# Casting q and k from a packed order: contiguous reads and strided writes in place of strided reads and contiguous writes

## The chip, the cores and the metric

The kernel runs on one core of a Trainium2 chip. Its time is the device time of one execution in microseconds (us). A core has TensorE (PE; its weight loads are listed apart as PEld), VectorE (DVE), ScalarE (ACT), GpSimd (POOL) and SyncE (SP). Each takes its instructions from a queue of its own in order, and they wait for one another with semaphores. SP issues most of the DMAs, GpSimd those of the FFN's weights, and ScalarE a few at the start.

## The reference

Two stages, for 4 batches, 8 heads, 768 tokens and a head dimension of 64.

First an attention that picks chunks. Keys are cut into 24 chunks of 32; for each chunk the minimum and the maximum of every key component are taken. A query's upper bound for a chunk is `sum(max(q*kmin, q*kmax))` over the 64 components. Chunks that lie behind the query's own are barred, the best 6 of the others are kept, and softmax attention runs over the kept chunks with a causal mask.

```
ub = sum(maximum(q * k_min, q * k_max), axis=-1)   # then the causal bar
sel = the 6 chunks with the highest ub
attn = softmax(where(sel & causal, q @ k.T / 8, -1e9))
x = (attn @ v) as 3072 tokens x 512
out = (silu(xn @ w_gate) * (xn @ w_val)) @ w_out,   xn = x / rms(x) * rms_g
```

Then a gated FFN with RMS norm: 3072 tokens, 512 wide, 1536 inside. The output is 3072 x 512 in float32.

## The kernel before

The work is cut into 12 blocks, each of one batch and 256 tokens (`ORDER`); the first four blocks are token block 0 of batches 0 to 3, where only 8 chunks exist. A block has two groups `g` of four heads. Blocks are counted from 0 here.

**Order of the work.** Every step (a few instructions on one engine) is registered with `plan.op` or `flex` (where more than one engine could do it), with estimated costs and a due time from the list `DUE`. `Plan.run` simulates engines and DMA rings with these estimates and writes out one order for each engine before the kernel is built. The order in which steps are issued thus follows from the estimates, not from what happens on the chip. The planner also writes filler matmuls (`keep_busy`, L1245) into PE's queue where it expects a gap in the first 60 us.

**The packed order.** For the blocks in `PACKED` (0, 1, 2) q and k are loaded so that one partition row `r` (of 32) holds 8 neighbouring tokens `j`: token = 8 r + j. VectorE's transpose of 32x32 squares (`turn`, L794) then leaves `kT` and `qT` as `[128, 2, 256]` float32 with the 256 columns in the order (j, r): a packed order. For the other blocks token = 32 j + r, so the same transpose leaves the columns in natural order.

From `kT` and `qT`, for each group:

- `half` (L801 on ScalarE, L802 on GpSimd) casts to bf16 into `kb` and `qb`, in natural token order. These feed the score matmuls `S` (L922). In packed blocks it reads `order(...)`, that is r outside and j inside, so that neighbouring reads are 32 float32 elements apart, and writes one after the other.
- `ext` (L809, VectorE) takes the minimum and the maximum of each chunk into `kx`; `dk` (L815) subtracts; `bd` (L834) places the results in `BO`, the weights of the upper bound.
- `relu` (L888, GpSimd or VectorE) writes max(q, 0) of the last 64 tokens over the first part of `qraw`, in packed blocks in natural order, reading with the same stride.
- `upper_first` (L698, PE) multiplies `qT` and that relu with `BO` for the blocks of token block 0. Its moving operand is read in the order (r, j): from `qT` with a rearranged pattern, from the relu as it lies.

What follows: `ubn`, `top`, `mk`, `mt` and `swap` on VectorE (some of `swap` on ScalarE, L759) pick chunks and build the mask; score matmuls and mask matmuls (L922, L933), exponentials (L972, ScalarE), the causal triangle (L942, GpSimd), values (L998, PE), division (L1013, L1017, VectorE) into `xnat`; then the norm: squares (L1034, ScalarE), the root (L1040, L1042, GpSimd), scaling `xs` (L1068 ScalarE, L1066 VectorE), transposes on PE (L1078) and `xsT` (L1087 ScalarE, L1091 VectorE). The FFN takes `xsT` as its moving operand (L1122), then tanh (L1129), products (L1133, L1141, L1144) and the projection (L1169). The FFN of block i is issued beside the attention of later blocks.

Buffers: `kT` and `qT` have 2, `qraw` 3, `qb` 5, `kb` 17; PSUM has four `F` banks and two `S` pairs. The weights come in nine loads of 512 KB from GpSimd's queue, the first of them behind the `dk` of block 0, with L942 between them.

Of the kernel before, what the change touches and what calls it, by code (L numbers as in the profile page):

```python
# [11 lines left out]
ACT = mybir.ActivationFunctionType  # L12
# [395 lines left out]
def kernel(  # L408
# [41 lines left out]
    def at(key):  # L450
        return store[plan.pool_of[key]][plan.slot[key]]
# [46 lines left out]
    VE, SE, GE, TE, SY = nc.vector, nc.scalar, nc.gpsimd, nc.tensor, nc.sync  # L498
# [13 lines left out]
    PACKED = {0, 1, 2}  # L512
# [27 lines left out]
    def flex(name, alts, pri, **kw):  # L540
        e = next(iter(alts))
        o = plan.op(name, e, *alts[e], pri, **kw)
        o.alts = alts
        return o
# [102 lines left out]
    def pick(i, gs):  # L647
        b, m = ORDER[i]
        w = 64 if m == 0 else BLK
# [10 lines left out]
        def own_(key):  # L660
            return [key + (g,) for g in gs]
# [4 lines left out]
        def bank():  # L666
            return [at(x)[:, 0:n * 32 * nj].rearrange("p (g n) -> p g n", g=n) for x in ub]
# [16 lines left out]
        def upper_first():  # L684
            for k_, g in enumerate(gs):
                qT, qr, bo = sides[i, g][0:3]
                x = at(qT)[:, g]
                if i in PACKED:
                    x = x.rearrange("p h (j r) -> p h r j", r=32)[:, :, 32 - w // 8:].rearrange(
                        "p h (c r) j -> p h c r j", c=2)  # L690
                else:
                    x = x[:, :, BLK - w:].rearrange("p h (c r j) -> p h c r j", c=2, j=8)
                qs = [x, qr().rearrange("p h (c r j) -> p h c r j", c=2, j=8)]
                d = at(bo)
                for t in range(4):
                    for hp in range(2):
                        for c in range(2):
                            TE.matmul(bank()[hp][64 * c:64 * (c + 1), k_].rearrange("p (r j) -> p r j", j=8),  # L698
                                      d[64 * hp:64 * (hp + 1), t, :],
                                      qs[t // 2][64 * hp:64 * (hp + 1), t % 2, c],  # L700
                                      start=(t == 0), stop=(t == 3),
                                      skip_group_check=True)

        reads = []
        for g in gs:
            qx, qr, bd, qR, qraw, crossed = sides[i, g]
            reads += [bd, qx, qR, qraw] + crossed
            if m:
                reads += [bd + (x,) for x in range(m + 1)] + [qx + (g,)]
        o = plan.op(f"upper{tag}", "PE", (0.52 if m else 0.49) * n, (0.52 if m else 0.49) * n + 0.165,  # L710
                    upper if m else upper_first, base + 3, reads=reads, writes=ub, takes=[(x, "F") for x in ub])
        o.mode = "sq"

        def rows(key):
            return at(key)[:, g0:g1].rearrange("p g h j c -> p (g h) j c")

        def flat(key):
            return at(key)[:, g0:g1].rearrange("p g h j c -> p g h (j c)")[:, :, :, 0:32 * nj]

        turned = ((0.37 if m else 0.17), (0.65 if m else 0.25))[n - 1]  # L720
# [14 lines left out]
        def top():  # L735
# [10 lines left out]
            out=rows(mk)[:, :, 0:nj], in0=rows(ubn)[:, :, 0:nj],  # L746
# [3 lines left out]
            out=flat(mtd), in_=flat(mk)), base + 3, reads=[mk] + own_(mk), writes=own_(mtd),  # L750
# [17 lines left out]
    def job(i, g):  # L768
        b, m = ORDER[i]
        J = (b, m, g)  # L770
        w = 64 if m == 0 else BLK
# [6 lines left out]
        def turned(nm):  # L778
            return at(kT) if nm == "k" else at(qT)[:, g]

        packed = i in PACKED

        def order(x):

            return x.rearrange("p h (j r) -> p h r j", r=32) if packed else x

        def natural(x):
            return x.rearrange("p h (r j) -> p h r j", r=32) if packed else x
        bd = ("BD", b)

        def turn(nm):
# [6 lines left out]

        def half(nm):
            T, hb = kT if nm == "k" else qT, (nm + "b", *J)  # L800
            act = lambda: SE.activation(out=natural(at(hb)), in_=order(turned(nm)), func=ACT.Copy)  # L801
            pool = lambda: GE.tensor_copy(natural(at(hb)), order(turned(nm)))  # L802
            flex(f"half {nm}{J}", {"ACT": (0.54, 0.63, act), "POOL": (0.57, 0.61, pool)},
                 base + 2 - first, reads=[T, T + (g,)], writes=[hb], takes=[(hb, nm + "b")])

        turn("k")
        half("k")
        for n, op in enumerate((ALU.min, ALU.max)):
            plan.op(f"ext{n}{J}", "DVE", 0.585, 0.67, lambda n=n, op=op: VE.tensor_reduce(  # L809
                out=at(kx)[:, g, n], in_=at(kT).rearrange("p h (j c x) -> p h c j x", j=8, x=4)  # L810
# [21 lines left out]
        for n in range(0 if m else 2):  # L832
            def put(eng, n=n):
# [8 lines left out]
                 writes=[bo + (n,)], takes=[] if n else [(bo, "BO")])  # L842
        turn("q")
        half("q")
        qR, qx = ("qR", *J), ("QX", b, m)

# [6 lines left out]
        if m:  # L853
# [6 lines left out]
            if i in BYRING:  # L860
                crossed = [qx + (n, "x") for n in range(4)]
                for n, (lo, hi, p_, t) in enumerate(CROSS if g == NG - 1 else ()):
                    o = plan.op(f"qm{n}({b}, {m})", "SP", 0.57, 0.57,
                                lambda lo=lo, hi=hi, p_=p_, t=t: SY.dma_start(
                                    out=at(qx)[hi:hi + 32, :, p_, BLK - w:], in_=at(qT)[lo:lo + 32, :, t, BLK - w:]),
                                base - 20, reads=[qT, qx] + [x + (y,) for x in (qT, qx) for y in range(NG)],
                                writes=[qx + (n, "x")])
# [9 lines left out]
        def qr():  # L877
            return at(qraw)[:, g].rearrange("p j h d -> p (j h d)")[:, 0:2 * w].rearrange(
                "p (h s) -> p h s", h=2)

        def relu(eng):
            def go():
                o, x = qr(), at(qx if m else qT)[:, g]
                if packed:
                    o, x = o.rearrange("p h (r j) -> p h r j", j=8), order(x)[:, :, 32 - w // 8:]
                else:
                    x = x[:, :, BLK - w:]
                eng.tensor_scalar(out=o, in0=x, scalar1=HUGE, scalar2=0.0, op0=ALU.min, op1=ALU.max)  # L888
            return go
# [21 lines left out]
        def unit(kg, sc, tiles, masked):  # L911

            kbt, qbt = at(("kb", b, kg, g)), at(qb)
            s = [at(x) for x in sc]
            for e, q0, q1, c0 in tiles:
                ks = slice(P * e, P * (e + 1))
                jq = max(j0, q0 // 64)
                mask = masked and jq < q1 // 64
                for t in range(2):
                    for a in range(4):  # L920
                        r = slice(32 * a, 32 * (a + 1))
                        TE.matmul(s[a // 2][:, a % 2, c0:c0 + q1 - q0],  # L922
                                  kbt[r, t, ks], qbt[r, t, q0:q1],
                                  start=(t == 0), stop=(t == 1 and not mask), skip_group_check=True)
                for d in range(2) if mask else ():
                    for a in range(4):
                        r = slice(32 * a, 32 * (a + 1))
                        hp = a // 2
                        c = hp if d == 0 else 1 - hp
                        o = s[hp][:, a % 2, c0:c0 + q1 - q0].rearrange(  # L930
                            "p (j c r) -> p j c r", c=2, r=CH)[:, jq - q0 // 64:, c, :]
                        mv = (at(mtd)[r, g, hp] if d == 0 else at(mto)[r, g])[:, jq - j0:nj, :]
                        TE.matmul(o, chunkrow[r, BLK * kg + P * e:BLK * kg + P * (e + 1)], mv,  # L933
                                  start=False, stop=(d == 1), skip_group_check=True)
# [11 lines left out]
        for kg in [m] + list(range(m)):  # L946
# [11 lines left out]
            for part, tiles, c0, c1, pe, occ, lat in parts:  # L958
# [4 lines left out]
                o = plan.op(f"scores{J}{kg}{part}", "PE", pe, pe + 0.2,  # L963
                            lambda kg=kg, sc=sc, tiles=tiles, masked=masked: unit(
                                kg, sc, tiles, masked), pri,
                            reads=[("kb", *jk), qb] + ([mtd, mto, mtd + (g,), mto + (g,), "chunkrow"] if masked else []),
                            writes=sc, takes=[(x, "S") for x in sc])
                o.mode = "row"
                for hp in range(2):
# [3 lines left out]
                                out=at(pt)[:, hs, c0:c1], in_=at(x)[:, :, c0:c1], func=ACT.Exp,  # L973
# [13 lines left out]
        for s in range(2):  # L987
# [3 lines left out]
            def values(s=s, av=av, nkb=nkb):  # L991
                o = at(av)[:, 0:4 * (D + 1)].rearrange("p (a d) -> p a d", a=4)
                for kb_ in range(nkb):
# [3 lines left out]
                    for a in range(4):  # L997
# [7 lines left out]
            o = plan.op(f"values{J}{s}", "PE", 0.129 * nkb, 0.129 * nkb + 0.16, values, pri,  # L1005
                        reads=have + [("VX", b, x, g) for x in range(m + 1)],
                        writes=[av], takes=[(av, "F")])
            o.mode = "full"

            def view(av=av):  # L1010
# [7 lines left out]
                        out=at(xn)[:, g * 256:(g + 1) * 256].rearrange("p (a d) -> p a d", a=4),  # L1018
# [260 lines left out]
```

## Time and profile before

| | us |
|---|---|
| runs | 299.69, 300.06, 302.14; median 300.06 |
| profiled execution: span from first to last instruction | 297.4 |
| the same with what lies around the span | not recorded for that execution; the runs' median lies 2.7 above its span |
| PE busy / ScalarE busy / GpSimd busy | 282.5 / 216.7 / 155.6 |
| twelve packed casts: ten on ScalarE, two on GpSimd | 1.06 to 1.15 each |
| six packed relus on GpSimd | 0.40 each |

How rows are read. A group of instructions has the source line, the engine, the operation, output<-input with shapes, and the count; then busy time and the mean of one in ns; then the idle time of the engine ahead of these instructions and what ended it. Rows of the timeline begin with the start and the duration in us; neighbouring instructions of the same kind are merged. The chain of waits begins at the last instruction and is followed back to what released each step. Rows on waiting say who waited for whom, and for how long in total, how often, and at most.

### The profile page before, as it was taken

The numbers are of one execution on the slowest core, as the hardware profiler recorded it, in microseconds if no ns is written. First come the engines' busy times: TensorE is split into PE (matmuls) and PEld (weight loads), VectorE is DVE, ScalarE is ACT, GpSimd is POOL, SyncE is SP. The second block draws the span as 40 slices with busy tenths as digits, with TensorE's granted clock in tenths as the row PEclk, the third lists the DMA queues.
The fourth block names the chain that finished last, engine by engine and source line by source line (L and its number), as shares of the span: only waits on it lengthen the run. The fifth ranks groups of instructions, "written<-read, shape, count | busy, mean of one in ns | idle before, by whom it ended". The sixth has DMA issues, their size and how long they took to land.

```text
span 297.4 us, 11418 instructions
## 1 busy us (share of the span) xinstructions
PE 282.5 (95%) x4672; PEld 213.4 (72%) x4672; DVE 217.1 (73%) x623; ACT 216.7 (73%) x372; POOL 155.6 (52%) x266
## 2 busy tenths in 40 slices
PE   7879999999999996999999999899999999999994
PEld 7548777657858854878767787488688778678763
DVE  6987774977998998888999999679356454456430
ACT  4897877688979876987985797677587668565331
POOL 4885858755976864475583276538044114214120
PEclk9999999999999999999999999999999999999998
DMA  7999998755676656654768576511014021011011
GB/s 188 208 204 206 255 197 163 159 130 134 141 194 154 144 136 103 149 100 110 205 135 162 108 193 150 133 40 39 0 57 55 1 82 30 2 73 35 2 71 71
DMA packets 86388, 35.08 MB, mean 118 GB/s; under 512 B 74816, under 2 KB 81728, under 8 KB 86336
## 3 DMA queue, kind: packets, MB, share of 16 engines
q1 hardware_dynamic: 80736, 29.12, 42.6%
q0 software_dynamic: 4752, 4.72, 9.4%
q8 instruction: 36, 0.59, 0.8%
q10 hardware_dynamic: 848, 0.53, 0.7%
q14 instruction: 16, 0.13, 0.2%
HBM read 28.58 MB, written 6.29 MB: 117 GB/s over the span
## 4 chain that ended last, share of the span: by engine, by line
PE 76%; DMA 9%; DVE 4%; ACT 4%; SPq 3%; POOL 1%; issue 1%; DVEq 0%; POOLq 0%; ACTq 0%
PE F L1122 39%; PE F L1169 18%; PE S L922 6%; PE F L998 6%; PE F L680 3%; SPq L528 3%; PE S L933 2%; DMA xsT<-xs 2%; DMA qraw<-in_q_dram 2%; DMA vraw<-in_v_dram 2%; DMA kraw<-in_k_dram 2%; DVE kx L809 1%; POOL hh L1144 1%; DVE m L739 1%; ACT th L1129 1%
## 5 line engine op out<-in xcount | busy, mean ns | idle before, releaser
L972 ACT ACTIVATE pt<-S 128x1024 bf16<-128x1024 f32 (+3 forms) x104 | 85.6, 857 | 19.7 <-PE S L933 18.2
L1144 POOL TENSOR_TENSOR hh<-tg,vs 128x512 bf16<-128x512 bf16 x48 | 55.7, 1164 | 42.6 <-ACT vs L1141 22.9
L1133 DVE SCALAR_TENSOR_TENSOR tg<-th,F 128x512 bf16<-128x512 bf16 x72 | 48.4, 680 | 39.3 <-ACT th L1129 33.7
L1122 PE MATMUL F<-xsT,wg 128*128 128x256 bf16 (+1 forms) x608 | 72.6, 267 | 3.7 <-DVE xnat L1017 1.7
L1122 PE MATMUL F<-xsT,wv 128*128 128x256 bf16 (+1 forms) x608 | 72.4, 267 | 0.6 <-DMA xsT<-xs 0.3
L1169 PE MATMUL F<-wo,hh 128*128 128x512 bf16 (+1 forms) x300 | 68.5, 371 | 1.8 <-POOL hh L1144 0.6
L1122 PEld LDWEIGHTS <-wg 128*128 128x128 bf16 x608 | 55.6, 98 | 13.5 <-issue 2.7
L1122 PEld LDWEIGHTS <-wv 128*128 128x128 bf16 x608 | 55.2, 98 | 9.7 <-DMA vraw<-in_v_dram 0.8
L1129 ACT ACTIVATE th<-F 128x512 bf16<-128x512 f32 x72 | 42.5, 598 | 19.7 <-PE F L1122 17.4
L942 POOL TENSOR_SCALAR_AFFINE_SELECT pt<-pt 128x512 bf16<-128x512 bf16 x48 | 32.2, 674 | 32.3 <-ACT pt L972 31.7
L1169 PEld LDWEIGHTS <-hh 128*128 128x128 bf16 x300 | 27.7, 98 | 28.4 <-issue 1.8
L1141 ACT ACTIVATE vs<-F 128x512 bf16<-128x512 f32 x48 | 28.7, 598 | 13.2 <-PE F L1122 10.1
L922 PE MATMUL S<-qb,kb 32*128 32x256 bf16 (+1 forms) x800 | 32.8, 253 | 2.3 <-ACT qb L801 2.0
L809 DVE TENSOR_REDUCE kx<-kT 128x16 f32<-128x512 f32 x48 | 30.4, 664 | 0.0
L998 PEld LDWEIGHTS <-pt 128*128 128x128 bf16 x672 | 24.8, 98 | 3.1 <-issue 0.3
L998 PE MATMUL F<-VX,pt 128*128 128x65 bf16 x672 | 26.6, 194 | 0.2 <-ACT vs L1141 0.2
L922 PEld LDWEIGHTS <-kb 32*128 32x128 bf16 x800 | 13.9, 92 | 15.0 <-issue 14.4
L933 PE MATMUL S<-mtd,chunkrow 32*128 32x128 bf16 (+2 forms) x384 | 20.5, 203 | 0.2 <-issue 0.2
L933 PE MATMUL S<-mto,chunkrow 32*128 32x128 bf16 (+2 forms) x384 | 19.9, 203 | 0.0
L1017 DVE TENSOR_TENSOR xnat<-F,rden 128x256 bf16<-128x256 f32 x48 | 19.2, 415 | 0.7
L933 PEld LDWEIGHTS <-chunkrow 32*128 32x128 bf16 x768 | 18.5, 93 | 1.2 <-issue 0.4
L1034 ACT ACTIVATE junk<-xnat 128x512 bf16<-128x512 bf16 x24 | 15.1, 631 | 5.4 <-DVE xnat L1017 5.0
(71 smaller groups left out, 337.2 us busy)
## 6 DMA issues: line engine op xcount, KB each, us to landing
vraw<-in_v_dram SPq DMA_DIRECT2D x24, 256.0 KB, 4.4
out_dram<-osb SPq DMA_DIRECT2D x23, 256.0 KB, 2.4
kraw<-in_k_dram SPq DMA_DIRECT2D x72, 64.0 KB, 2.4
qraw<-in_q_dram SPq DMA_DIRECT2D x72, 64.0 KB, 2.2
QX<-qT SPq DMA_DIRECT2D x32, 64.0 KB, 2.7
wg<-in_moe_w_gate_dram POOLq DMA_DIRECT2D x3, 512.0 KB, 12.3
wv<-in_moe_w_val_dram POOLq DMA_DIRECT2D x3, 512.0 KB, 14.3
wo<-in_moe_w_out_dram POOLq DMA_DIRECT2D x3, 512.0 KB, 23.5
```

Of the source, the lines that this page charges most:

```text
L809: plan.op(f"ext{n}{J}", "DVE", 0.585, 0.67, lambda n=n, op=op: VE.tensor_reduce(out=at(kx)[:, g, n], in_=at(kT).rearrange("p h (j c x) -> ...
L922: TE.matmul(s[a // 2][:, a % 2, c0:c0 + q1 - q0], kbt[r, t, ks], qbt[r, t, q0:q1], start=(t == 0), stop=(t == 1 and not mask), skip_group_ ...
L933: TE.matmul(o, chunkrow[r, BLK * kg + P * e:BLK * kg + P * (e + 1)], mv, start=False, stop=(d == 1), skip_group_check=True)
L942: GE.affine_select(out=d, in_=d, compare_op=ALU.is_ge, fill=0.0, base=0, pattern=[[0, 4], [1, P]], channel_multiplier=-1)
L972: lambda pt=pt, hs=hs, c0=c0, c1=c1, x=sc[hp]: SE.activation(out=at(pt)[:, hs, c0:c1], in_=at(x)[:, :, c0:c1], func=ACT.Exp, scale=SCALE), ...
L998: TE.matmul(o[:, a, :], p_[:, a, off:off + P], vt[:, e, a, :], start=(kb_ == 0 and a == 0), stop=(kb_ == nkb - 1 and a == 3), skip_group_c ...
L1122: TE.matmul(at(p_)[:, n * W:(n + 1) * W], w[:, g, ht * P:(ht + 1) * P], at(xT)[:, g, x0:x0 + W], start=(g == 0), stop=(g == NP - 1), skip_ ...
L1129: plan.op(f"tanh{U}.{hp}", "ACT", 0.48, 0.6, lambda th=th, gp=gp: SE.activation(out=at(th), in_=at(gp), func=ACT.Tanh, scale=0.5), pri - 0 ...
L1133: VE.scalar_tensor_tensor(out=at(tg), in0=at(th), scalar=1.0, in1=at(gp), op0=ALU.add, op1=ALU.mult), pri - 30, reads=[th, gp], writes=[tg ...
L1141: plan.op(f"vcopy{U}.{hp}", "ACT", 0.48, 0.6, lambda vs=vs, vp=vp: SE.activation(out=at(vs), in_=at(vp), func=ACT.Copy), pri + 0.1, reads= ...
L1144: plan.op(f"hh{U}.{hp}", "POOL", 1.11, 1.16, lambda tg=tg, vs=vs, hh=hh: GE.tensor_tensor(out=at(hh), in0=at(tg), in1=at(vs), op=ALU.mult) ...
L1169: TE.matmul(at(op)[:, cs], at(key)[:, o:o + P], wo[:, ht, cs], start=(ht == 0), stop=(ht == NHT - 1), skip_group_check=True)
```

## The change

Three places follow the packed order now. The casts go through `kT` and `qT` in memory order (j outside, r inside) and write each element to its natural place, so that neighbouring writes are 8 bf16 elements (16 bytes) apart, in runs of 32. The relu also goes by (j, r) and leaves its result packed, reading 8 neighbouring elements at a time. The upper bound matmuls therefore read the relu's result with a rearranged pattern, as they do for `qT`. Estimates, due times, buffers and DMAs are as before, and so is the order of instructions on every engine. One line is added ahead of all lines named above from L698 on, so that L801 becomes L802, L802 becomes L803, L888 becomes L889, L1122 becomes L1123.

```diff
-                qs = [x, qr().rearrange("p h (c r j) -> p h c r j", c=2, j=8)]
+                qs = [x, qr().rearrange("p h (j c r) -> p h c r j" if i in PACKED else
+                                        "p h (c r j) -> p h c r j", c=2, j=8)]
...
-        def order(x):
+        def by_line(x):
-            return x.rearrange("p h (j r) -> p h r j", r=32) if packed else x
+            return x.rearrange("p h (j r) -> p h j r", r=32) if packed else x
         def natural(x):
-            return x.rearrange("p h (r j) -> p h r j", r=32) if packed else x
+            return x.rearrange("p h (r j) -> p h j r", r=32) if packed else x
...
-            act = lambda: SE.activation(out=natural(at(hb)), in_=order(turned(nm)), func=ACT.Copy)
-            pool = lambda: GE.tensor_copy(natural(at(hb)), order(turned(nm)))
+            act = lambda: SE.activation(out=natural(at(hb)), in_=by_line(turned(nm)), func=ACT.Copy)
+            pool = lambda: GE.tensor_copy(natural(at(hb)), by_line(turned(nm)))
...
-                    o, x = o.rearrange("p h (r j) -> p h r j", j=8), order(x)[:, :, 32 - w // 8:]
+                    o, x = o.rearrange("p h (j r) -> p h j r", j=8), by_line(x)[:, :, :, 32 - w // 8:]
```

## The prediction

> **What bounds the kernel now.** I read the busy times first, then the windows, then ScalarE's work in the windows where the change sits, and the chain of waits last.
>
> From the page of before:
>
> ```profile
> span 297.4 us, 11418 instructions
> PE 282.5 (95%) x4672; PEld 213.4 (72%) x4672; DVE 217.1 (73%) x623; ACT 216.7 (73%) x372; POOL 155.6 (52%) x266
> ```
>
> And three windows of it; the columns are the length, then busy time and instruction count for PE, PEld, DVE, ACT and POOL, then the granted clock, the DMA share and GB/s:
>
> ```profile
> 0.00:22.90 22.90, 18.45 (x350) 13.39 (x351) 18.32 (x56) 17.56 (x33) 16.84 (x60) 1.00 1.03 200
> 22.90:46.00 23.10, 21.96 (x383) 18.38 (x382) 17.77 (x53) 17.76 (x37) 15.53 (x24) 1.00 1.20 224
> 46.00:297.40 251.40, 242.09 (x3945) 181.67 (x3942) 180.97 (x516) 181.41 (x304) 123.23 (x182) 1.00 0.43 101
> ```
>
> PE is busy 95% of the span, so over most of it the end is set by PE. The exception is the first 22.9 us. There PE looks busy at 18.45 us, but much of that is filler (the matmuls of L1245 on constants), and the first matmul of the FFN only comes at 22.85, as PE's timeline has it:
>
> ```profile
> 22.85 1.07 PE L1122 MATMUL F<-xsT,wg 128*128 128x128 bf16 x16
> ...
> 34.80 1.91 PE L1122 MATMUL F<-xsT,wg 128*128 128x256 bf16 x16
> ```
>
> Whatever moves that first matmul moves nearly everything behind it, because from there PE idles for only 1.14 us up to 46 (23.10 less 21.96). All casts that the change touches lie before 41 us. So the question is how far they reach the PE queue at about 23 us and at about 39 us.
>
> The casts themselves, grouped by shape: ScalarE in block 0 (5.7 to 10.1 us), block 1 (13.6 to 22.3) and block 2 (34 to 40), GpSimd in block 2 (34 to 46), and then the same casts in later blocks, which read and write in memory order:
>
> ```profile
> L801 ACT ACTIVATE kb<-kT 128x512 bf16<-128x512 f32 x2 | 2.1, 1094 | 1.6 <-DVE kT L794 1.6
> ...
> L801 ACT ACTIVATE qb<-qT 128x512 bf16<-128x512 f32 x2 | 2.2, 1098 | 0.0
> L801 ACT ACTIVATE kb<-kT 128x512 bf16<-128x512 f32 x2 | 2.2, 1097 | 0.5 <-DVE kT L794 0.5
> ...
> L801 ACT ACTIVATE kb<-kT 128x512 bf16<-128x512 f32 x1 | 1.1, 1115 | 0.0
> ...
> L802 POOL CAST kb<-kT 128x512 bf16<-128x512 f32 x1 | 1.1, 1062 | 0.0
> L888 POOL TENSOR_SCALAR qraw<-qT 128x128 f32<-128x128 f32 x2 | 0.8, 400 | 0.5 <-DVE qT L794 0.5
> ...
> L801 ACT ACTIVATE kb<-kT 128x512 bf16<-128x512 f32 x9 | 5.5, 629 | 0.6 <-DVE kT L794 0.5
> ...
> L802 POOL CAST kb<-kT 128x512 bf16<-128x512 f32 x9 | 5.5, 609 | 4.2 <-DVE kT L794 3.9 <-DVE rden L1013 0.3
> L888 POOL TENSOR_SCALAR qraw<-qT 128x128 f32<-128x128 f32 x2 | 0.6, 292 | 0.8 <-DMA kraw<-in_k_dram 0.7
> ```
>
> The reader is to see the price of the strided read: 1094 ns against 629 on ScalarE, 1062 against 609 on GpSimd. Over 512 elements that is 0.9 ns more for each, on either engine. The relu pays 400 against 292 ns, 0.84 ns for each of 128 elements. So one element at a time, 128 bytes apart, costs 0.9 ns over the packed rate, and this is what the change takes away on the reading side.
>
> **The change part by part.** The instruction order of every engine is unchanged (the planner's costs and due times are not touched), no DMA and no wait is added or taken away; only addresses inside instructions differ.
>
> *Casts.* There are 12, two k and two q in each of three blocks: ten on ScalarE, two on GpSimd. Reads become contiguous: 0.46 us less for each. Writes become single bf16 elements 16 bytes apart, in runs of 32 that then start over 2 bytes on. No row of before has a strided bf16 write of any length, so I bound it. From below: if a write costs the same wherever it goes, the cast falls to 0.63 us. The nearest row in that direction:
>
> ```profile
> L905 ACT ACTIVATE VX<-vraw x10: 615/632/647, 10.5 to 186.2; 128x512 bf16<-128x512 f32 x10
> ```
>
> It writes runs of 64 elements with a gap of one behind each, at the packed price; but these are still runs. In the middle: a lone write costs as much as a lone read, and the cast stays at about 1.09 us. From above I take the slowest elementwise bf16 instruction of the trace per element, which is VectorE's:
>
> ```profile
> 2.17 2.28 DVE L566 TENSOR_SCALAR chunkrow<-pat 128x768 bf16<-128x768 bf16 x1
> ```
>
> 2.28 us over 768 elements is 2.97 ns each; 512 of those are 1.52 us, 0.43 us more than now. It is another engine and another pattern, so this is only an end. I take the middle, 1.09 us: the strided reads and the strided writes have in common that neighbouring accesses don't share a word, and reads pay the same 0.9 ns on two engines of different design (0.91 on ScalarE, 0.88 on GpSimd), which points to the memory and not to the engine. Then each strided cast is worth nothing, on either side of the path.
>
> The Trainium skill ("Vector Engine (DVE) Microarchitecture Reference", section "Measured stream behaviour on trn2") says that a port streams at full rate only in runs of at least two adjacent 4-byte words, and lists a destination hopping every element at 1.71 ns a column beside 1.73 for a source doing so and 1.054 packed; by that rule the casts stay where they are and the sum is 0. The same table has 2.50 ns for a destination stepping 24 words, and by an estimate from that figure (512 times 2.50, some 1.4 us with the fixed cost) this change would lose. That is the rule that speaks against it; the trace's own step of 32 words shows 1.7 to 1.8 ns on the reading side (the packed 0.83 ns of the page plus 0.9), so it sides with the lower figure so far, and no row shows it for writes.
>
> *Relu.* Six instructions on GpSimd; reads become runs of eight adjacent elements. 400 falls to about 292 ns, 0.11 us each. It is hidden: in block 1 the engine waits for VectorE soon after (the row below, with 0.30 us of idle time in brackets), in block 0 the step behind the two relus is the same subtraction of VectorE's results, and in block 2 the rows above have 0.5 us of idle time before the relus. I count it at nothing; if that cover were gone, it is 0.22 us in a block.
>
> ```profile
> 20.74 0.22 POOL L815 TENSOR_TENSOR kx<-kx 128x16 f32<-128x16 f32 x1 [0.30 <-DVE rden L1013]
> ```
>
> *Upper bound matmuls (L698).* Half of those of the packed blocks, 96, now read the relu's output 32 bytes apart. The trace has both kinds side by side, in blocks 0 to 2:
>
> ```profile
> L698 PE MATMUL F<-qT,BO x96: 226/227/248, 10.3 to 44.1; 64*64 64x32 f32 x96
> L698 PE MATMUL F<-qraw,BO x96: 218/219/227, 10.6 to 44.3; 64*64 64x32 f32 x96
> ```
>
> The strided qT costs 8 ns more than the contiguous qraw from start to end, and they overlap: in the chain shown below, 26 of both kinds take 0.66 us, 25 ns each. On a wait for the last one it is 8 ns a group, and if none of it overlapped, 96 times 8 ns or 0.8 us, spread over three blocks. Taken: 0.
>
> *Sum* for the likeliest case: 297.4 us of span plus 0. The runs' median of 300.06 lies 2.7 us above the span; nothing outside the span changes, so the time is 300.0.
>
> **What a cheaper or dearer write would do: the path.** ScalarE's timeline in block 1 (start, duration; the idle time before, with its releaser, in brackets):
>
> ```profile
> 13.71 1.10 ACT L801 ACTIVATE kb<-kT 128x512 bf16<-128x512 f32 x1 [0.46 <-DVE kT L794]
> ...
> 15.67 1.09 ACT L801 ACTIVATE kb<-kT 128x512 bf16<-128x512 f32 x1
> 16.66 0.63 ACT L1034 ACTIVATE junk<-xnat 128x512 bf16<-128x512 bf16 x1
> ...
> 18.22 1.09 ACT L801 ACTIVATE qb<-qT 128x512 bf16<-128x512 f32 x1
> 19.19 0.73 ACT L1068 ACTIVATE xs<-xnat,ri_all 128x512 bf16<-128x512 bf16 x1
> 19.80 1.11 ACT L801 ACTIVATE qb<-qT 128x512 bf16<-128x512 f32 x1
> 20.80 0.39 ACT L972 ACTIVATE pt<-S 128x256 bf16<-128x256 f32 x1
> 21.06 1.15 ACT L1087 ACTIVATE xsT<-F,rmsg 128x128 bf16<-128x128 bf16 x4
> ```
>
> From 13.71 to the end of xsT at 22.21 there is no gap: four casts are in series with the square, the scaling and the xsT that the first FFN matmul needs. The chain of waits, though, enters this stretch from elsewhere:
>
> ```profile
> 17.06 0.71 DVE qT L794
> ...
> 18.88 0.62 DVE qT L794
> ...
> 21.21 0.11 DVE BO L834
> 21.32 0.91 ACT xsT L1087 x3
> 22.27 0.66 PE F L698 x26
> ...
> 34.26 0.71 ACT junk L1034 x2
> 34.97 1.01 ACT kb L801
> ...
> 36.59 0.97 ACT th L1129 x2
> 37.57 1.04 ACT xsT L1087 x4
> 38.65 2.80 PE F L1122 x32
> ```
>
> So a faster cast soon meets VectorE. The q casts can't start before qT is there (17.77 and 19.50), and L698 needs the BO that ends at 21.32 whatever ScalarE does. A slower one meets nothing.
>
> **The rivals.**
>
> *Writes are free (0.63 us a cast).* Block 0 gains nothing: behind the casts PE's second group stands after L698 in the queue, which waits for BO. In block 1 the second q cast starts at 19.50 and ends at 20.1, the exponential at 20.4, xsT at 21.5 in place of 22.21; L698 then goes on at 21.55, after BO, in place of 22.27, and the first FFN matmul comes 0.6 us sooner. In block 2, kb saves 0.46 us ahead of xs, but the two tanh behind it wait for the matmuls of 34.80, which end at 36.71, so xsT gains 0.2. Together 0.8 us: 299.2. [...] Against it: the 0.9 ns look like the memory's, and the next gain is late at once, so even this is small.
>
> *Writes are dearer than the reads were (1.52 us a cast).* This is the case on the other side. In block 0 PE's first scores wait for the third cast, and the idle time there is ScalarE's doing:
>
> ```profile
> PE S L922 <- ACT qb L801: 2.0, 2, 1.1
> ```
>
> Three casts at 0.43 us more push it by 1.3 us, and with it L698, the picks on VectorE and kT, so the cast of 13.71 starts at 15.0; GpSimd's weight loads between its two selects (L942) go later with it. Four casts in block 1 add 1.7: the first FFN matmul is 3.0 us late. The kb of block 2 adds 0.4. 3.4 us, of which PE's 1.14 us of idle time up to 46 us could take some: 302.3 to 303.5, middle 303.0. It decides from the packed price: each 0.1 us by which a cast exceeds 1.09 costs some 0.8 us, while each 0.1 us below gives some 0.2.
>
> *The change doesn't do what it says*: the instructions are issued with the old order of elements, or reads cost as before and writes are added on top (1.09 plus 0.46, 1.55 us a cast). The built program names the casts with a four-dimensional pattern in place of a flat one, so the first is out; the second is the dearer case over again, 303.
>
> **How the numbers follow.** Middle case 0.47, range of its own 299.5 to 300.9 (0.9 to 1.2 us a cast: 0.2 per 0.1 down, 0.8 per 0.1 up); free writes 0.27, at 299.2; dearer writes 0.26, the two forms together, anywhere from 300.9 to 304. The range 298.9 to 303.2 holds the first two nearly whole and two thirds of the third. Within 1% is 297.06 to 303.06, about what a measurement can tell from no change. Faster by more than 1% needs 3 us, and the path has 0.8 to give: 0.02. Slower by more than 1% is the upper part of the dearer case: 0.11. Within: 0.87.
>
> **What the profile after would show.** The cast rows of L802 on ScalarE decide: near 1.09 us the middle case, near 0.63 the first rival, at 1.4 and above the second. The two GpSimd casts should go the same way from 1.06 and 1.07; the relu (L889) should read 0.29. L698's rows with qraw should rise from 219 to at most about 227 ns. The first FFN matmul (L1123) stands at 22.85 in the middle case, at about 22.2 with free writes, at about 25 or later with dear ones. The prediction is wrong if that matmul moves by another amount than the casts allow, if the window behind 46 us changes its length of 251.4 us by more than 0.5 us, or if the end moves without the casts.

## The result and the profile after

| | runs | median us | ratio to before |
|---|---|---|---|
| before | 4 | 300.79 (299.69 to 302.14) | |
| changed | 4 | 315.31 (314.43 to 315.99) | 1.048 (95%: 1.0448 to 1.0512) |

The kernel became 14.5 us slower. The profiled executions have spans of 297.4 and 313.1 us, 15.7 us apart. Runs of the kernel before spread from about 299 to 303 us, and its profiled execution lies at the low end: where a run's time and its span are both on record they differ by about 1.7 us, not by the 2.7 of the sum. One execution of the first run with more filler below was slow (317.69 us, 1.5% above the fastest of its kernel) and is left out.

First the same three windows as in the prediction, of the changed kernel (length, then busy time and count for PE, PEld, DVE, ACT and POOL, then granted clock, DMA share, GB/s):

```profile
0.00:22.90 22.90, 16.53 (x215) 12.15 (x216) 13.29 (x38) 16.48 (x17) 10.70 (x47) 0.85 1.06 211
22.90:46.00 23.10, 19.02 (x332) 14.74 (x330) 11.98 (x41) 19.29 (x34) 12.08 (x23) 0.78 1.21 227
46.00:313.10 267.10, 254.27 (x4130) 191.93 (x4127) 192.54 (x546) 192.99 (x323) 134.51 (x197) 1.00 0.40 94
```

Up to 22.9 us ScalarE started 17 instructions in place of 33 in about the same busy time, and PE's granted clock is 0.85 and then 0.78, where it was 1.00. The casts, grouped by shape (ScalarE 5 to 53 us, GpSimd 0 to 56 us):

```profile
L802 ACT ACTIVATE qb<-qT 128x512 bf16<-128x512 f32 x5 | 12.6, 2609 | 0.0
L802 ACT ACTIVATE kb<-kT 128x512 bf16<-128x512 f32 x5 | 12.3, 2555 | 2.6 <-DVE kT L795 2.6
...
L803 POOL CAST qb<-qT 128x512 bf16<-128x512 f32 x1 | 2.5, 2481 | 0.0
L803 POOL CAST kb<-kT 128x512 bf16<-128x512 f32 x1 | 2.5, 2462 | 0.0
```

A cast that reads in memory order and writes bf16 elements 16 bytes apart takes about 2.5 us, on both engines: 2.3 times the strided read (1.09) and four times the packed cast (0.63). The chain of waits in the first 28 us shows where that goes; it is now ScalarE's, where it was VectorE's and the DMAs':

```profile
5.13 0.72 DVE kT L795
...
5.88 4.79 ACT kb L802 x2
10.67 2.70 ACT qb L802 x2
...
14.73 0.71 ACT pt L973
...
19.76 2.50 ACT kb L802
...
23.16 2.39 ACT kb L802
...
27.04 2.37 ACT qb L802
```

And PE's timeline, with the idle time in brackets, followed by three windows with length, PE's busy time and count, clock, DMA share and GB/s:

```profile
12.98 0.29 PE L923 MATMUL S<-qb,kb 32*128 32x128 bf16 x8 [4.13 <-ACT qb L802]
...
29.45 0.40 PE L923 MATMUL S<-qb,kb 32*128 32x128 bf16 x8 [3.66 <-ACT qb L802]
...
34.48 1.89 PE L1123 MATMUL F<-xsT,wg 128*128 128x128 bf16 x16
...
52.63 1.05 PE L1123 MATMUL F<-xsT,wg 128*128 128x128 bf16 x16 [0.73 <-ACT xsT L1088]
```

```profile
5.00:12.90 7.90, 3.85 (x48) 1.00 1.12 224
12.90:22.00 9.10, 8.79 (x135) 0.62 1.23 220
...
29.40:38.30 8.90, 8.85 (x130) 0.51 1.19 234
```

The first FFN matmul moved from 22.85 to 34.48, 11.6 us; the one behind the second xsT of the same kind from 38.65 to 52.63, 14.0 us. After each of the two long gaps PE ran at about half its clock: the 16 matmuls at 34.48 took 1.89 us, where they took 1.07. The Trainium skill ("TensorE: Matmul & The Clock Gate", section "What's actually happening") has half the clock after an idle window of some 3.4 us; the gaps of 4.13 and 3.66 us agree with it. In a later run a wait of 2.2 us was followed by a clock of 0.59 too (under "PE's clock" below), which that figure does not explain.

### The profile page after: what moved, and what is told of

Its sections match the earlier page's. It is cut to its first block, busy times and chain, and to the rows that moved or that the text cites. A ratio compares the mean times of both kernels' runs of the same rounds, so it can differ in the third digit from the quotient of the medians.

```text
span 313.1 us, 11418 instructions
## 1 busy us (share of the span) xinstructions
PE 289.8 (93%) x4672; PEld 218.8 (70%) x4672; DVE 217.8 (70%) x623; ACT 228.8 (73%) x372; POOL 157.3 (50%) x266
## 4 chain that ended last, share of the span: by engine, by line
PE 67%; ACT 10%; DMA 7%; DVE 5%; SPq 5%; issue 3%; POOL 2%; ACTq 0%; DVEq 0%; POOLq 0%
PE F L1123 31%; PE F L1170 18%; PE S L923 6%; PE F L999 5%; ACT kb L802 4%; SPq L528 3%; DMA kraw<-in_k_dram 3%; PE F L680 2%; PE S L934 2%; ACT qb L802 2%; ACT pt L973 2%; SPq L865 2%; DMA QX<-qT 2%; PE F L1246 1%; PE F L699 1%
## 5 line engine op out<-in xcount | busy, mean ns | idle before, releaser
L973 ACT ACTIVATE pt<-S 128x1024 bf16<-128x1024 f32 (+3 forms) x104 | 86.5, 866 | 19.2 <-PE S L934 16.9
L1123 PE MATMUL F<-xsT,wg 128*128 128x256 bf16 (+1 forms) x608 | 73.4, 270 | 4.9 <-DMA xsT<-xs 1.7
L1123 PE MATMUL F<-xsT,wv 128*128 128x256 bf16 (+1 forms) x608 | 73.0, 269 | 0.2
L1123 PEld LDWEIGHTS <-wg 128*128 128x128 bf16 x608 | 56.4, 99 | 14.7 <-issue 3.9
L1123 PEld LDWEIGHTS <-wv 128*128 128x128 bf16 x608 | 56.0, 99 | 9.1 <-issue 0.8
L943 POOL TENSOR_SCALAR_AFFINE_SELECT pt<-pt 128x512 bf16<-128x512 bf16 x48 | 31.3, 655 | 41.2 <-ACT pt L973 40.8
L923 PE MATMUL S<-qb,kb 32*128 32x256 bf16 (+1 forms) x800 | 33.6, 257 | 8.6 <-ACT qb L802 7.8
L1142 ACT ACTIVATE vs<-F 128x512 bf16<-128x512 f32 x48 | 28.7, 600 | 12.4 <-PE F L1123 9.0
L802 ACT ACTIVATE kb<-kT 128x512 bf16<-128x512 f32 x14 | 17.8, 1317 | 3.3 <-DVE kT L795 3.1
```

The costliest lines, as they stand in the source:

```text
L802: act = lambda: SE.activation(out=natural(at(hb)), in_=by_line(turned(nm)), func=ACT.Copy)
L923: TE.matmul(s[a // 2][:, a % 2, c0:c0 + q1 - q0], kbt[r, t, ks], qbt[r, t, q0:q1], start=(t == 0), stop=(t == 1 and not mask), skip_group_ ...
L943: GE.affine_select(out=d, in_=d, compare_op=ALU.is_ge, fill=0.0, base=0, pattern=[[0, 4], [1, P]], channel_multiplier=-1)
L973: lambda pt=pt, hs=hs, c0=c0, c1=c1, x=sc[hp]: SE.activation(out=at(pt)[:, hs, c0:c1], in_=at(x)[:, :, c0:c1], func=ACT.Exp, scale=SCALE), ...
L1123: TE.matmul(at(p_)[:, n * W:(n + 1) * W], w[:, g, ht * P:(ht + 1) * P], at(xT)[:, g, x0:x0 + W], start=(g == 0), stop=(g == NP - 1), skip_ ...
```

## The experiments

**Which part of the change.** Three kernels put one part of it into the kernel before, and a fourth leaves only the relu and the upper bound matmuls.

Relu and upper bound matmuls alone:

```diff
-            act = lambda: SE.activation(out=natural(at(hb)), in_=by_line(turned(nm)), func=ACT.Copy)
+            act = lambda: SE.activation(out=old_out(at(hb)), in_=old(turned(nm)), func=ACT.Copy)
```

(`old` and `old_out` are `order` and `natural` of the kernel before; the cast on GpSimd likewise.)

> Casts as before (strided reads, contiguous writes); only the relu keeps the packed order, and the upper bound matmuls read it strided. Theory A (the 15 us come from the bf16 casts' strided writes alone): within 1 us of before, the relu at 0.29 us, the casts at 1.09 us, L699 as in before where the clock is full. Rival B (the strided moving operand of the upper bound matmuls, or the relu, has a part in it: L699 took 270 ns at the median in the changed kernel against 227): at least 2 us slower than before.

Measured: 300.23 us beside 300.70, ratio 0.9989 (0.9963 to 1.0014). Its relu (L895) and its upper bound matmuls, grouped as before:

```profile
L895 POOL TENSOR_SCALAR qraw<-qT 128x128 f32<-128x128 f32 x6 | 1.8, 293 | 4.6 <-DVE qT L801 4.6
```

```profile
L699 PE MATMUL F<-qT,BO x96: 226/227/248, 10.5 to 44.4; 64*64 64x32 f32 x96
L699 PE MATMUL F<-qraw,BO x96: 227/233/238, 10.7 to 44.6; 64*64 64x32 f32 x96
```

So theory A holds against B: this part is worth nothing that can be told from the noise (the interval is 1.1 us faster to 0.4 us slower). The longer L699 of the changed kernel went with the low clock: up to 46 us these matmuls took 291 ns there at the median, and in block 2, at a clock of 1.00, 227 ns (qT) and 233 ns (relu).

The casts of one block alone, here block 0; 1 and 2 alike:

```diff
+        def src(x):
+            return x.rearrange("p h (j r) -> p h j r", r=32) if i == 0 else order(x)
+        def dst(x):
+            return x.rearrange("p h (r j) -> p h j r", r=32) if i == 0 else natural(x)
...
-            act = lambda: SE.activation(out=natural(at(hb)), in_=order(turned(nm)), func=ACT.Copy)
+            act = lambda: SE.activation(out=dst(at(hb)), in_=src(turned(nm)), func=ACT.Copy)
```

> The kernel before, with only block 0's four casts written strided. Theory A with the casts in series: four casts of 2.48 us in place of 1.09, 5.6 us, less the 0.3 to 0.8 us of idle time that ScalarE has behind them, plus what PE's clock loses after the longer gap before the first scores (0 to 1 us): 4.5 to 6.5 us slower. Rival C (the first 23 us wait for DMAs anyway, and the casts of block 0 hide under the loads): under 2 us slower.

> The kernel before, with only block 1's four casts written strided. Theory A: four casts in a stretch of ScalarE without gaps, 5.6 us, and the first FFN matmul that much later; a gap of some 3 us before the scores of block 1 may cost PE its full clock as in the changed kernel (1 to 2 us): 5 to 7.5 us slower. If the clock costs nothing: 5 to 5.6.

> The kernel before, with only block 2's four casts written strided, two on ScalarE and two on GpSimd. Theory A: only the k cast that stands ahead of xs is on the path, and the q cast behind xsT in part: 1.4 to 3 us slower; GpSimd's two hide. If the three blocks add up to the whole, the three differences sum to about 15 us.

| strided writes in | median us | less before's 300.70 | ratio |
|---|---|---|---|
| block 0 | 306.52 | 5.8 | 1.0202 (1.0163 to 1.024) |
| block 1 | 306.15 | 5.4 | 1.0184 (1.0128 to 1.024) |
| block 2 | 301.87 | 1.2 | 1.0045 (1.0029 to 1.0061) |

Theory A holds in blocks 0 and 1; C falls, since nothing of block 0's casts is seen to hide under the loads. Block 1's 5.4 us also lie in the 5 to 5.6 expected if the clock costs nothing, so that run does not tell the two apart. Block 2 came in just under the expected 1.4 to 3. The three sum to 12.4 us of the whole's 14.5. The 2.1 us left over are not clear of the noise: the intervals are 1.2 us each way for block 0, 1.7 for block 1, 0.5 for block 2 and 1.0 for the whole. In the profiled executions nothing is missing up to about 50 us. The matmul behind the second xsT stands at 38.65 before and at 52.63 in the changed kernel; with block 0, 1 or 2 alone it comes here:

```profile
45.51 1.05 PE L1128 MATMUL F<-xsT,wg 128*128 128x128 bf16 x16 [0.73 <-ACT xsT L1093]
...
44.95 1.05 PE L1128 MATMUL F<-xsT,wg 128*128 128x128 bf16 x16 [0.73 <-ACT xsT L1093]
...
40.10 1.05 PE L1128 MATMUL F<-xsT,wg 128*128 128x128 bf16 x16 [0.72 <-ACT xsT L1093]
```

These are 6.9, 6.3 and 1.5 us later than before, 14.6 in all, against 14.0 in the changed kernel.

**What a write costs.** A kernel with nothing but copies of 512 float32 elements of each partition and the writing of the output:

```diff
+    case("b16_step16B", BF16, 1, 8)    # name, type, run of adjacent elements, step of runs
...
+            for name, (t, run) in cases.items():
+                eng(t[:, :, 0:run], src.rearrange("p (n r) -> p n r", r=run))
```

> A kernel that leaves the whole computation out and writes zeros: it only copies 512 float32 elements of each partition into tiles of several patterns, three times on each of ScalarE, GpSimd and VectorE, to time the write by itself. Theory D (a write that fills only a part of a 4-byte word is dear by itself): bf16 in lone elements costs about 2.5 us at every step from 4 to 32 bytes, bf16 in runs of 2 and more about 0.6 to 1.1, float32 in lone elements at most about 1.1 like the strided read. Rival E (each hop to another 16-byte line is dear): bf16 at a step of 4 or 8 bytes is well under 2.5, float32 at a step of 16 or 32 bytes is about 2.5 as well. Rival F (it is the kernel's pattern, which goes back 2 bytes further after 32 elements): only the pattern of the casts is at 2.5, a plain step of 16 bytes is cheaper.

ScalarE's rows, from one execution (b for bf16, f for float32; ns min/median/max of three; `b_cast` has the pattern of the changed kernel's casts, `read128B` the strided read of before):

```profile
L47 ACT ACTIVATE b_packed<-src x3: 612/612/631, 3.7 to 40.0; 128x512 bf16<-128x512 f32 x3
L47 ACT ACTIVATE b_step4B<-src x3: 752/752/759, 4.2 to 40.5; 128x512 bf16<-128x512 f32 x3
L47 ACT ACTIVATE b_step8B<-src x3: 1314/1348/1354, 4.8 to 43.2; 128x512 bf16<-128x512 f32 x3
L47 ACT ACTIVATE b_step16B<-src x3: 2513/2516/2528, 5.9 to 46.5; 128x512 bf16<-128x512 f32 x3
L47 ACT ACTIVATE b_step32B<-src x3: 2666/2696/2701, 7.9 to 48.5; 128x512 bf16<-128x512 f32 x3
L47 ACT ACTIVATE b_run_step32B<-src x3: 612/613/614, 11.5 to 52.1; 128x512 bf16<-128x512 f32 x3
L47 ACT ACTIVATE f_step8B<-src x3: 646/649/651, 12.5 to 53.1; 128x512 f32<-128x512 f32 x3
L47 ACT ACTIVATE f_step16B<-src x3: 1097/1134/1138, 13.1 to 53.9; 128x512 f32<-128x512 f32 x3
L47 ACT ACTIVATE f_step32B<-src x3: 1129/1132/1133, 14.0 to 54.9; 128x512 f32<-128x512 f32 x3
L47 ACT ACTIVATE b_cast<-src x3: 2453/2493/2499, 15.4 to 59.6; 128x512 bf16<-128x512 f32 x3
L47 ACT ACTIVATE read128B<-wide x3: 1150/1158/1174, 17.4 to 61.6; 128x512 bf16<-128x512 f32 x3
```

None of the three theories survives whole. F falls: the casts' pattern is not dearer than a plain step of 16 bytes (2.49 and 2.52). D falls at the small steps: lone bf16 elements at 4 bytes cost 0.75, not 2.5. E falls with float32: at 16 and at 32 bytes it costs 1.13, about the price of the strided read, not 2.5. The rows of lone elements fit a price for each 16 bytes touched, one for bf16 and a lower one for float32. As an estimate: a contiguous copy takes 0.61 us for 512 elements and 0.41 for 256 (row L805 of the next experiment), so about 0.2 us of each instruction is fixed. Less that, lone bf16 elements pay 4.5 ns for each 16 bytes touched, at a step of 16 bytes (2.32 us for 512 places) as at 8 (1.15 us for 256), and 4.9 ns at 32; lone float32 elements at 16 or 32 bytes pay 1.8 ns (0.93 us for 512); runs of 8 bf16 pay nothing over the packed copy. Two more patterns, runs of 2 and of 4 bf16 at a step of 16 bytes, stand under one name, since the view leaves numbers out of names. The first row is runs of 2 alone, the second the mean of both, so that runs of 4 took 606 ns:

```profile
L47 ACT ACTIVATE b_run_step16B<-src 128x512 bf16<-128x512 f32 x1 | 0.9, 934 | 0.0
...
L47 ACT ACTIVATE b_run_step16B<-src 128x512 bf16<-128x512 f32 x2 | 1.4, 770 | 0.0
```

A pair of bf16 fills a whole 4-byte word and still pays 2.9 ns for each of 256 places (0.73 us), between the two prices; runs of 4 pay nothing over the packed copy. So a half-filled word is not the whole rule. The rows show these prices; what makes the narrow element dear, they do not show.

The Trainium skill ("Vector Engine (DVE) Microarchitecture Reference", section "Measured stream behaviour on trn2") gives its prices for 32-bit elements, measured on VectorE: 1.71 ns a column for a destination hopping 4 KiB at every element, 2.50 for one stepping 24 words. The float32 rows of ScalarE here are near the first (1.8 ns by the estimate above); the lone bf16 rows at 16 and 32 bytes (4.5 and 4.9 ns) are near neither, and no row here has a step of 24 words.

**Whether the time on ScalarE is all.** No strided write, but as much time ahead of each of ScalarE's packed casts:

```diff
+                if packed:
+                    SE.activation(out=natural(junk.rearrange("p (h x) -> p h x", h=2)),
+                                  in_=order(turned(nm)), func=ACT.Copy)
+                    SE.activation(out=spare[:], in_=turned(nm)[:, 0], func=ACT.Copy)
                 SE.activation(out=natural(at(hb)), in_=order(turned(nm)), func=ACT.Copy)
```

> The kernel before, casts and all accesses as they were, but ahead of each of ScalarE's ten packed casts stand two more copies of the same input into unused tiles (512 elements with the strided read, 256 contiguous), some 1.3 us of issue time in place of the 1.39 us that the strided write adds. No write is strided. Theory I (the 15 us are the casts' time on ScalarE, in series, and what PE's gaps do to its clock; the strided writes disturb nobody else): 11.5 to 15 us slower than before, the first FFN matmul at about 33 to 34 us. Rival J (the writes also hold up other engines' access to SBUF): at most 9 us slower.

Measured: 314.96 us, ratio 1.045 (1.0395 to 1.0506), with the first FFN matmul here:

```profile
34.19 1.89 PE L1127 MATMUL F<-xsT,wg 128*128 128x128 bf16 x16
```

That is the changed kernel again (1.048; 34.48, at the same half clock); the matmul behind the second xsT comes at 52.29, there at 52.63. Theory I holds, J falls: both matmuls lie 0.3 us from those of the changed kernel, so the time that the casts take on ScalarE is enough for the effect, and no cost of the strided writes to other engines shows beside it. The copies stand in for that time only roughly (some 1.3 us for 1.39), and the intervals of the two times at the end (1.7 and 1.0 us each way) would hide a smaller cost. The casts and the added copies in this run, grouped (for kT; those for qT are alike):

```profile
L805 ACT ACTIVATE spare<-kT 128x256 bf16<-128x256 f32 x5 | 2.0, 405 | 0.0
L806 ACT ACTIVATE kb<-kT 128x512 bf16<-128x512 f32 x5 | 5.4, 1077 | 0.0
```

**PE's clock.** More filler in the gaps of the changed kernel:

```diff
+                if n > 0 and f:
+                    n += MORE.get(self.warmed, 0)    # MORE = {0: 60, 6: 15}
+                    self.warmed += 1
```

> The changed kernel with more filler matmuls in PE's queue at the two places where it waits for the casts: 60 more small ones before the first scores, 15 more wide ones before the scores of block 1. Theory G (PE's clock falls to half after these gaps and so costs a part of the 15 us): the granted clock stays near 1.0, and the kernel is 1.5 to 4 us faster than the changed one, so still 11 to 13.5 us slower than before. Rival H (PE waits for ScalarE either way, so the clock costs nothing): within 0.7 us of the changed kernel, 14 to 15.5 us slower than before.

> As the run with more filler, with a few more (66 small, 3 and 16 wide). The last one had the first FFN matmul 1.8 us and the first output tile 3.3 us earlier than the changed kernel, and lost both between 113 and 166 us, where PE waited 2.2 us in one place and its clock fell again. If that loss is chance: 311 to 314 us. If PE's clock in the first 40 us is worth nothing at the end: 315 to 316 again.

Measured: 315.31 us (312.94 to 316.72, three executions) and 313.48 us (312.41 to 314.82, four); ratios to before 1.0487 (1.0433 to 1.0541) and 1.0394 (1.033 to 1.0458), where the changed kernel has 315.31 us and 1.048 (1.0448 to 1.0512). The granted clock stayed at 1.00 through 46 us in both, and the first FFN matmul came 1.8 us sooner; the first run's row and then its windows further on:

```profile
32.71 1.07 PE L1130 MATMUL F<-xsT,wg 128*128 128x128 bf16 x16
```

```profile
165.00:167.50 2.50, 0.32 (x14) 1.00 0.71 141
167.50:170.00 2.50, 2.50 (x12) 0.59 0.55 128
```

In the profiled execution of the first run the gain did not reach the end: at 165 us PE waits 2.2 us for VectorE (below: in total, times, longest, from 124 to 176 us), and the clock falls there, where the changed kernel has 1.00 in each 10 us from 120 to 180.

```profile
PE F L1130 <- DVE xnat L1025: 3.1, 2, 2.2
```

By their medians the two runs end level with the changed kernel and 1.8 us ahead of it, and all three intervals overlap. Neither G nor H is settled: the clock costs 1.8 us at the first FFN matmul, and at the end something between nothing and some 2 us.

**A version that beats both?** Two were tried. First, the q casts contiguous on both sides, with the score matmuls reading `qb` 64 bytes apart:

```diff
+                        if "q" in LIE and i in PACKED:
+                            qq = qbt[r, t].rearrange("p (j r) -> p r j", r=32)[:, q0 // 8:q1 // 8]
+                            oo = oo.rearrange("p (r j) -> p r j", j=8)
```

> The kernel before, with the q casts of blocks 0 to 2 neither reading nor writing strided: qb keeps the packed order, and the score matmuls of these blocks read it 64 bytes apart as their moving operand. k casts as before. This is the free write of my first rival for six of twelve casts. My accounting of the path: q casts fall to 0.63 us, the first FFN matmul comes 0.3 to 0.6 us sooner, 0 to 0.8 us faster than before if PE reads strided bf16 for nothing. Rival: PE pays for the strided read in the score matmuls (256 or 128 columns), which stand 2.5 times longer, and the kernel is slower than before.

Measured: 303.34 us beside 300.33, ratio 1.01 (1.0072 to 1.0128): 3 us slower. PE's score matmuls, before and then here, ns min/median/max up to 60 us:

```profile
L922 PE MATMUL S<-qb,kb x128: 211/214/278, 9.2 to 53.0; 32*128 32x128 bf16 x112, 32*128 32x256 bf16 x16
```

```profile
L930 PE MATMUL S<-qb,kb x128: 369/388/604, 8.6 to 55.5; 32*128 32x128 bf16 x112, 32*128 32x256 bf16 x16
```

The q casts fell to 0.64 us and the first FFN matmul came at 22.56 in place of 22.85: 0.3 us, as the path was accounted. But PE pays for the stride in each score matmul, 1.8 times where the rival had 2.5, and PE is the bound from there on: the last of the 128 starts at 55.5 in place of 53.0. The rival holds.

Second, VectorE's transposes write natural order at once, and all that follows is contiguous:

```diff
-                    lambda: VE.transpose(out=turned(nm).rearrange("p h (j r) -> p j h r", r=32, j=8),
+                    lambda: VE.transpose(out=turned(nm).rearrange("p h (r j) -> p j h r" if lie else
+                                                                  "p h (j r) -> p j h r", r=32, j=8),
...
-        packed = i in PACKED
+        packed, lie = False, i in PACKED
```

> A third way: VectorE's transposes of blocks 0 to 2 write the natural order at once (float32 in lone elements 32 bytes apart), so that casts, relu and upper bound matmuls are all contiguous. By the table of writes a float32 copy of 512 elements with such a destination takes VectorE about 0.3 us more than a packed one. Casts 0.63 us each, transposes 1.0 in place of 0.7; the q transposes stand on the chain at 17 to 20 us, so two of them cost 0.6 us there and the casts give 0.6: within 1 us of before. If the transposes pay nothing for it: 0.5 to 1 us faster than before. If they pay like lone bf16 (2 us and more): 5 us slower.

Measured: 301.63 us beside 301.20, ratio 1.0012 (0.9981 to 1.0043): no difference, as the first of the three cases had it. The transposes before and in this kernel, and then its casts:

```profile
L794 DVE STREAM_TRANSPOSE qT<-qraw x6: 670/700/712, 7.3 to 38.6; 128x512 f32<-128x512 f32 x6
...
L794 DVE STREAM_TRANSPOSE qT<-qraw x6: 1076/1098/1115, 7.5 to 39.4; 128x512 f32<-128x512 f32 x6
```

```profile
L802 ACT ACTIVATE qb<-qT 128x512 bf16<-128x512 f32 x5 | 3.2, 630 | 2.2 <-DVE qT L794 2.2
L802 ACT ACTIVATE kb<-kT 128x512 bf16<-128x512 f32 x5 | 3.1, 628 | 3.0 <-DVE kT L794 3.0
```

VectorE pays 0.40 us more for a transpose (1.10, from 0.70) and ScalarE gets 0.46 back for a cast. In float32 the stride cost about the same in the three places where it was measured: 0.46 us in ScalarE's read, 0.40 in VectorE's transpose, and 0.52 in ScalarE's write of the table (1.13 against 0.61 packed).

## Why the prediction was wrong

**The step that failed** is the price of the cast. The prediction took 1.09 us for a lone write, on the ground that lone reads pay the same 0.9 ns on two engines and so the memory sets the price, for writes too. It measured 2.46 to 2.61 us. ScalarE and GpSimd agree again in the kernel (2.55 to 2.61 and 2.46 to 2.48), but that the memory sets the price is not shown: in the table of writes the casts' pattern took 2.49 us on ScalarE, 2.86 on GpSimd and 2.15 on VectorE. What the prediction left out is the width: the reads are of 4-byte elements, the writes of 2-byte ones, and by the table the 4-byte write would have cost 1.13, close to what was assumed. The reads' row could not tell what a 2-byte write costs.

**The upper bound failed with it.** 1.52 us was the slowest elementwise row of the trace for each element, and nothing made it a bound for a pattern that the trace doesn't contain. The range took it for an end, and the end was 1 us short for each of twelve casts.

**The path was right in kind, and its sizes came out near in part by luck.** Its 0.8 us for each 0.1 us counts eight casts. At ScalarE's mean of 2.58 us that is 1.49 times 8, 11.9 us, against 14.5 measured; seven of them come before the first FFN matmul, 10.4 us, against 11.6. In block 0 the path is longer than was said: the fourth cast stands on it too, because the exponential behind it on ScalarE (9.99 before, 14.73 after) is what the next scores wait for (0.23 us at 15.48); the chain above runs through both. In exchange, casts that follow one another overlap in part (two take 4.79 us in the chain), so that one adds less than 1.49 us. The rows are the exponential before and block 1's first cast in the first run with more filler:

```profile
9.99 0.63 ACT L972 ACTIVATE pt<-S 128x256 bf16<-128x256 f32 x2
...
18.38 2.49 ACT L809 ACTIVATE kb<-kT 128x512 bf16<-128x512 f32 x1 [0.46 <-DVE kT L802]
```

That cast started at 13.71 before and starts at 19.76 in the changed kernel, 6.1 us later. With more filler, at a clock of 1.00, it is 4.7 us: the four casts. The other 1.4 us went with the low clock behind PE's gap of 4.13 us, a price that the prediction didn't give to a wait. Up to the first FFN matmul it is the same: 9.9 us with the clock kept, 11.6 without. How much of this reaches the end stays open.

**A sign that could not tell.** The window behind 46 us grew from 251.4 to 267.1 us, which was set down as a sign of being wrong. It has a fixed start, so that a dearer cast lengthens it like any other delay.

**Right:** that the relu and the upper bound matmuls are worth nothing that shows (0.9989; 400 to 293 ns, 219 to 233 ns, which is 6 ns above the 227 that was set as the most), that GpSimd's two casts hide (block 2 in all costs 1.2 us, no more than the one cast of ScalarE that was counted there), and the direction of the dearer rival, with ScalarE's casts ahead of PE's first scores as its place. That a free write would bring little is borne out only for the q casts and at the first FFN matmul (0.3 us with the casts at 0.64); no kernel had all casts packed at no price elsewhere.

**The chances** gave the dearer case 0.26 and its time 303. With no row for a strided bf16 write, the case had no end that the trace could set, and the range should have said so.

## What to carry to other kernels

Moving a stride from the read to the write is not neutral where the write is narrower than the read: on ScalarE lone bf16 writes 16 bytes apart cost 2.5 us for 512 elements here, lone float32 reads 128 bytes apart or writes 16 bytes apart 1.1 us, runs of 4 or 8 bf16 elements 0.6 us. If a permutation has to be paid for on ScalarE, these rows say to pay for it on the float32 side, or in runs of at least 4 adjacent bf16 elements. And where no row of a trace has the pattern, time the pattern by itself before the price is put into a sum.

## What the runs showed of the hardware that was not expected

- ScalarE's lone bf16 writes get dearer with the step up to 16 bytes (0.75, 1.35, 2.52 us at 4, 8, 16 bytes) and hardly after that (2.70 at 32).
- VectorE does not follow the same table: lone bf16 at 16 bytes takes it 3.55 us, at 32 bytes 2.01, and the casts' pattern 2.15, where GpSimd takes 2.86 (below, from the same run; other engines were at work beside it, and these prices were not taken alone).

```profile
L51 DVE CAST b_step16B<-src 128x512 bf16<-128x512 f32 x3 | 10.6, 3550 | 0.0
...
L51 DVE CAST b_step32B<-src 128x512 bf16<-128x512 f32 x3 | 6.0, 2011 | 0.0
...
L52 DVE CAST b_cast<-src 128x512 bf16<-128x512 f32 x3 | 6.5, 2152 | 0.0
...
L52 POOL CAST b_cast<-src 128x512 bf16<-128x512 f32 x3 | 8.6, 2861 | 0.0
```

- A wait of PE of 2.2 us was followed by a granted clock of 0.59 (the first run with more filler, at 165 us), as waits of 3.66 and 4.13 us were by 0.51 and 0.62.
- A bf16 moving operand read 64 bytes apart costs PE 388 ns in place of 214 for 128 columns, where float32 at 128 or 32 bytes cost 8 and 14 ns more for 32 columns (227 and 233 against 219).
